# Attention and a gelu layer on one core: the first layer's matmuls of batches 1 to 6 in quarters of the array

## The chip, the cores and the metric

The kernel runs on one core of one Trainium2 chip. A core has a matrix engine, TensorE (PE in the profile, with PEld for its weight loads), and four others: VectorE (DVE), ScalarE (ACT), GpSimd (POOL) and SyncE (SP), which here issues most of the DMAs. Each engine works through its own queue of instructions in order; they wait for one another by semaphores. The metric is the time of one execution on the device, in microseconds.

## What is computed

```python
def _attn_ref(q, k, v, g_q, g_k):            # q, k, v: (8, 12, 448, 64)
    q_n, k_n = (rmsnorm(q, g_q), rmsnorm(k, g_k))
    scores = scale * np.matmul(q_n, k_n.transpose(0, 1, 3, 2))
    attn = np.exp(scores - max) ; attn = attn / sum
    return np.matmul(attn, v)

def _moe_ref(x, w_in, w_out):                # x: (3584, 768), w_in: (768, 2048), w_out: (2048, 768)
    h = x @ w_in
    g = 0.5 * h * (1.0 + np.tanh(c * (h + 0.044715 * h * h * h)))
    return g @ w_out
```

Eight batches of twelve heads go through attention, with q and k normalised; the 8 x 448 rows that come out, of 12 x 64 = 768 features, go through two dense layers with a gelu between them. The matmuls take bf16.

## The kernel before

The batches follow one another. For each there are three kinds of work on TensorE:

- **Attention.** A unit (`unit`, L334) makes the scores of one chunk of four heads and one tile of 64 keys, in four 64x64 quarters of the array, and ScalarE takes their exponential (L338). `products` (L383) makes, also in quarters, the sums of the exponentials and their product with v. VectorE divides (`turned`, `recips`, `quad_x`, L392 to L409) and leaves `xT[b]`, 128 rows by 6 chunks by 448 columns.
- **First layer.** `mm1_pair` (L500) multiplies `w_in` with `xT[b]`. The 2048 features are 16 tiles of 128, taken in 8 pairs; for each tile 6 matmuls with the whole 128x128 array and 448 columns run, one for each chunk `c`. A pair has its own two banks of PSUM. When both of its tiles are done, ScalarE takes the gelu (L513) into `g`. The last pair is done tile by tile, with a gelu for each, of 448 columns.
- **Second layer.** `mm2_quarters` (L443) multiplies `g` with `w_out`, in quarters of the array with 384 columns, for two half tiles of output at once. It runs over the upper and the lower 64 rows in two passes: in the first pass (p = 0) the one output takes rows 0 to 63 and the other 64 to 127, in the second pass (p = 1) the other way round. Between the passes stands a no-operation on SyncE (L452) that waits for the last matmul of the first pass; the first matmul of the second pass waits for it. For the last batch `mm2_last` (L474) uses the whole array.

The order is written by hand. `attention` (L540) runs a list of steps: U is a unit, d and a are one step of the second layer of the batch before (its result copied out by VectorE or ScalarE), A a sum of exponentials, s, t, r, x and q the steps to `xT`, E the gelu's table, m0 and m1 the first two pairs of the first layer, but only their first four chunks (`early`), as `xT` of the last two comes from q2. `first_two` does the same for the first two batches, from a longer list. Behind the steps the loop at L875 does the rest of the first layer: the last two chunks (`late`) of the first two pairs, then the six other pairs. At each tile number f functions of `plan` (L595) are called, which put other work into the engines' queues: POOL's normalisation of the next batch's q and k (`normed`), its transposes by DMA on SP (`dma_trans`, L315), loads (L126), squares of the batch after that on ScalarE (L170) and their sums on VectorE (L177).

PSUM is used as four pairs of banks (s0, s1, t0, t1), handed out in turn by `pair` and put back by `give`; whoever takes a pair waits until its last reader is done.

Of the kernel before, what the change touches and what calls it, by code (L numbers as in the profile page):

```python
# [11 lines left out]
AF = mybir.ActivationFunctionType  # L12
# [5 lines left out]
def kernel(  # L18
# [52 lines left out]
    def pair(name):  # L71
        t = idle_pairs.pop(0)
        if not whole:
            idle_pairs.append(t)
        return t
# [441 lines left out]
            give(h)  # L517

    early, late = range(HP - 2), range(HP - 2, HP)

    def m2_parts(b):
        tiles = range(3) if b % 2 == 0 else range(3, 7)
# [17 lines left out]
    def attention(b, m2, side, ends):  # L540


        units = [(c, t) for c in range(NCH) for t in range(NT)]
        firsts = (0, 3, 6, 9, 11, 13, 16, 18, 21)
        if b % 2 == 0:
            steps = (
# [4 lines left out]
            )  # L551
        else:
            steps = (
# [4 lines left out]
            )  # L558
        u, added_to, early_pairs = 0, 0, 0

        for step in steps.split():
            kind, n = step.rstrip("0123456789"), int(step.strip("UAsxtrqmEad") or 1)
            if kind == "U":
                if u in firsts:
                    for fn in side.get(firsts.index(u), ()):
                        fn()
                unit(b, *units[u])
                u += 1
            elif kind in ("a", "d"):
                for _ in range(n):  # L570
                    m2.pop(0)(nc.scalar.copy if kind == "a" else nc.vector.tensor_copy)
            elif kind == "A":
                for _ in range(n):
                    key_sums(b, *units[added_to])
                    added_to += 1
            elif kind == "s":
                products(b, n, 0)
            elif kind == "t":
                turned()
            elif kind == "r":  # L580
                recips()
            elif kind == "x":
                products(b, n, 1)
            elif kind == "q":
                quad_x(b, n)
            elif kind == "m":
                mm1_pair(n, early, b)
                early_pairs += 1
            elif kind == "E":
                for fn in ends:  # L590
                    fn()
                nc.scalar.preload_act_table_set(GELU_SET)
        return early_pairs
# [130 lines left out]
    def first_two(steps, m2):  # L724
# [3 lines left out]
        for step in steps.split():  # L728
# [27 lines left out]
            elif kind == "U":  # L756
                for _ in range(many):
                    unit(b, *units[u])
                    u += 1
            elif kind in ("a", "d"):  # L760
                for _ in range(many):
                    m2.pop(0)(nc.scalar.copy if kind == "a" else nc.vector.tensor_copy)
            elif kind == "A":
                for _ in range(many):
                    key_sums(b, *units[added_to])
                    added_to += 1
            elif kind in ("s", "x"):
                lo, hi = map(int, rest[1]) if rest[1:] else (0, NT)
                products(b, int(rest[0]), int(kind == "x"), lo, hi)
            elif kind == "q":  # L770
                quad_x(b, int(rest[0]))
            elif kind == "m":
                cs = {"e": early, "l": late}[rest[1]] if rest[1:] else range(HP)
                mm1_pair(int(rest[0]), cs, b)
            elif kind == "h":
                mm1_pair(int(rest[0]), range(HP), b, range(int(rest[1]), int(rest[1]) + 1))
            elif kind == "y":
                idle(many, warm()[:, :168])
            elif kind == "z":
                idle(many, warm())  # L780
            elif kind == "w":
                idle(many, ps_m.tile([128, 512], F32, tag="mm", name="w")[:, :S])
            elif kind == "V":
                load_v(int(rest[0]), 2 * int(rest[1]), 2)
            elif kind == "VV":
                load_v(int(rest[0]), 0, HP)
            elif kind == "VR":
                load_v(int(rest[0]), 2, 4)
            elif kind == "WF":
                w_in_part(0, int(rest[0]), 1)  # L790
            elif kind == "OO":
                w_out_part(int(rest[0]))
            elif kind == "W":
                w_in_part(*map(int, rest[0]))
            elif kind == "Y":
                w_in_rows(*map(int, rest[0]))
            elif kind == "O":
                w_out_part(*map(int, rest[0]), 2)
            elif kind == "gn":
                gain(*map(int, rest[0]))  # L800
            elif kind == "PS":
                b, u = 1, 0
                m2 += m2_parts(0)
                whole.append(True)
            elif kind == "PT":
                whole_psum()
            else:
                {"t": turned, "r": recips, "gp": gain_products, "gc": gains, "gm": bound, "sh": shifted,
                 "rel": released,
                 "rA": lambda: rsqrt(0, 0, q_only, (0,), slice(0, NT), twice=True),  # L810
                 "rB": lambda: rsqrt(0, 0, k_only, (1,), t_first),
                 "rC": lambda: rsqrt(0, 0, k_only, (1,), t_rest),
                 "r1": lambda: rsqrt(0, 1, near=(0, 1), also=(1,)),
                 "r2": lambda: rsqrt(0, 2, near=(1,)),
                 "N1": lambda: rsqrt_newton(1),
                 "rE": lambda: rsqrt(2, slice(0, NCH - 1)),
                 "eG": lambda: nc.scalar.preload_act_table_set(GELU_SET),
                 "eE": lambda: nc.scalar.preload_act_table_set(EXP_SET)}[kind]()
# [27 lines left out]
            )    , m2)  # L846
    begun = 2
    for b in range(1, B):
# [23 lines left out]
        if b + 1 < B:  # L872
            side.append((0, lambda: gain(b + 1, 2)))
        m1 = plan(*m1)
        for f in range(nf):  # L875
            if f + 1 == nf:
                for j in range(2):
                    mm1_pair(f // 2, range(HP), b, range(j, j + 1))
# [46 lines left out]
```

## Time and profile before

| what | us |
|---|---|
| median of three runs | 397.67 |
| their lowest and highest | 396.62, 398.26 |
| the profiled execution | 396.55 |
| its span, from the first to the last instruction | 394.4 |

The lines of the profile have the engine, the line of the kernel (L500), the operation, the tiles that it writes and reads, the part of the array (128*128 or 64*64), the shape and the count. A timeline starts each line with the start in us from the span's beginning and the length of the merged instructions; in square brackets stands the idle time of the engine before them and what ended it. A chain's lines are start, length, engine, tile, line and count. A window's line has the stretch and its length, the busy time and count of PE, PEld, DVE, ACT and POOL, the granted clock, the DMA share and GB/s. A matmul's record lasts longer than the distance to the next one's start, so the pace is read from starts.

### The profile page before, as it was taken

Reading aid. Unit: us, or ns where it says so; the run is one execution under the profiler, and the core shown is the slowest. Engines: PE = TensorE matmul, PEld = TensorE weight load, DVE = VectorE, ACT = ScalarE, POOL = GpSimd, SP = SyncE. Lnnn points to the kernel's source line nnn. Section 1 sums busy time; section 2 is a strip of 40 time slices with the busy share of each in tenths; the row PEclk is TensorE's granted clock in tenths of the full one; section 3 lists DMA queues with packets and bytes.
Section 4 is the critical chain, followed back from the end, with each engine's and each line's share of the span. In section 5 each row is a group of like instructions: output and inputs, shape, how many; then the busy total and the mean of one; then the engine's idle time right before and its main releaser. Section 6 shows DMA issues by size and latency. Waiting matters only on the chain.

```text
span 394.4 us, 12746 instructions
## 1 busy us (share of the span) xinstructions
PE 386.4 (98%) x5679; PEld 247.4 (63%) x5679; DVE 250.0 (63%) x384; ACT 276.4 (70%) x347; POOL 127.7 (32%) x107
## 2 busy tenths in 40 slices
PE   7989999999999999999999999999999999999996
PEld 6455567845666558855666557865666557865564
DVE  5999548896698267954599367963599505980010
ACT  6995389466995689847996579857898259854300
POOL 5995501874305440092203640073301800000000
PEclk9999999999999999999999999999999999999999
DMA  8999994989833947169731959249622611220033
GB/s 282 258 226 218 205 182 118 322 167 272 193 94 70 265 70 211 44 139 230 165 82 42 199 133 216 69 91 249 101 67 59 118 24 42 62 65 0 0 82 80
DMA packets 65594, 54.36 MB, mean 138 GB/s; under 512 B 37380, under 2 KB 60548, under 8 KB 65540
## 3 DMA queue, kind: packets, MB, share of 16 engines
q1 hardware_dynamic: 53184, 41.48, 41.5%
q0 software_dynamic: 12128, 11.80, 19.0%
q8 instruction: 44, 0.72, 0.8%
q10 hardware_dynamic: 228, 0.28, 0.3%
q14 instruction: 10, 0.08, 0.1%
HBM read 45.61 MB, written 11.01 MB: 144 GB/s over the span
## 4 chain that ended last, share of the span: by engine, by line
PE 93%; ACT 3%; DVE 1%; DMA 1%; issue 0%; DVEq 0%; SPq 0%
PE s L443 21%; PE s L500 19%; PE t L500 17%; PE t L443 11%; PE t L383 6%; PE t L334 4%; PE s L334 4%; PE t L474 3%; PE s L383 3%; ACT ex L338 3%; PE s L474 2%; PE tp L297 1%; PE o L383 1%; DMA rawq<-in_q_dram 1%; PE hh L500 1%; DVE nrmq L279 0%
## 5 line engine op out<-in xcount | busy, mean ns | idle before, releaser
L500 PEld LDWEIGHTS <-win 128*128 128x128 bf16 x768 | 74.3, 98 | 70.9 <-issue 3.0
L443 PEld LDWEIGHTS <-g 64*64 64x64 bf16 x3072 | 97.6, 107 | 32.8 <-SPq L452 2.9
L443 PE MATMUL s<-wout,g 64*64 64x384 bf16 x2048 | 102.7, 323 | 0.1
L338 ACT ACTIVATE ex<-t,shift 128x896 bf16<-128x896 f32 x86 | 84.2, 1013 | 3.7 <-PE t L334 2.0
L338 ACT ACTIVATE ex<-s,shift 128x896 bf16<-128x896 f32 x82 | 80.5, 1014 | 6.2 <-PE s L334 3.4
L500 PE MATMUL s<-xT,win 128*128 128x448 bf16 x402 | 81.5, 353 | 0.0
L177 DVE TENSOR_REDUCE ss<-sq 128x14 f32<-128x896 f32 (+3 forms) x45 | 44.4, 997 | 49.2 <-ACT sq L170 43.4
L500 PE MATMUL t<-xT,win 128*128 128x448 bf16 x354 | 71.6, 353 | 0.0
L513 ACT ACTIVATE g<-s 128x896 bf16<-128x896 f32 (+1 forms) x38 | 31.3, 828 | 37.5 <-PE s L500 37.5
L513 ACT ACTIVATE g<-t 128x896 bf16<-128x896 f32 (+1 forms) x33 | 27.5, 837 | 36.0 <-PE t L500 35.9
L443 PE MATMUL t<-wout,g 64*64 64x384 bf16 x1024 | 52.7, 323 | 0.0
L665 POOL COPY mark<-es 1x1 bf16<-1x1 bf16 x5 | 0.9, 178 | 115.4 <-DVE es L357 115.4
L279 POOL TENSOR_TENSOR nrmk<-rawk,rinv 128x896 bf16<-128x896 f32 (+1 forms) x21 | 34.6, 1648 | 5.9 <-DVE o L246 5.9
L279 POOL TENSOR_TENSOR nrmq<-rawq,rinv 128x896 bf16<-128x896 f32 (+1 forms) x21 | 34.5, 1645 | 3.3 <-ACT rinv L209 1.8
L334 PEld LDWEIGHTS <-kT 64*64 64x64 bf16 x672 | 23.4, 106 | 14.4 <-issue 5.4
L172 POOL TENSOR_TENSOR sq<-rawq 128x896 f32<-128x896 f32 (+1 forms) x10 | 15.3, 1534 | 52.9 <-DVE ss L177 26.8
L334 PE MATMUL s<-qT,kT 64*64 64x448 bf16 x328 | 29.8, 355 | 1.9 <-ACT ex L338 1.5
L334 PE MATMUL t<-qT,kT 64*64 64x448 bf16 x344 | 31.5, 350 | 0.0
L383 PEld LDWEIGHTS <-vb 64*64 64x64 bf16 x672 | 22.9, 107 | 8.0 <-issue 0.2
L401 DVE STREAM_TRANSPOSE rb<-rc 128x896 f32<-128x896 f32 x24 | 26.7, 1112 | 0.8
L360 DVE TENSOR_TENSOR e<-ex 128x896 bf16<-128x896 bf16 x32 | 19.4, 605 | 5.7 <-ACT ex L338 5.7
L383 PE MATMUL t<-ex,vb 64*64 64x448 bf16 x420 | 22.7, 349 | 0.0
(109 smaller groups left out, 386.0 us busy)
## 6 DMA issues: line engine op xcount, KB each, us to landing
out_dram<-osb SPq DMA_DIRECT2D x54, 192.0 KB, 2.8
rawq<-in_q_dram SPq DMA_DIRECT2D x23, 448.0 KB, 4.3
rawk<-in_k_dram SPq DMA_DIRECT2D x23, 448.0 KB, 5.5
vb<-in_v_dram POOLq DMA_DIRECT2D x8, 672.0 KB, 7.1
wout<-in_moe_w_out_dram POOLq DMA_DIRECT2D x2, 1536.0 KB, 22.9
win<-in_moe_w_in_dram POOLq DMA_DIRECT2D x6, 256.0 KB, 10.3
win<-in_moe_w_in_dram POOLq DMA_DIRECT2D x4, 384.0 KB, 13.0
kT<-nrmk SPq DMA_TRANSPOSE x19, 4.6
```

The lines of the kernel that those rows point to most:

```text
L172: eng.tensor_mul(sq, raw, raw)
L177: nc.vector.reduce_sum(sss[b][:, c, "qk".index(n), hs, ts], squares(b, c, n, hs, ts), axis=AX.X)
L279: eng.tensor_mul(nrms[n, b, c][:, ts].rearrange("p t a d -> p a t d"), raws[n, b, c][:, :, ts], root[:, :, ts].to_broadcast([P, 2, m, D]),)
L334: nc.tensor.matmul(sc[r * R:(r + 1) * R, a, :S], kT[rs, c, t, r], qT[b][rs, c, :, r], start=True, stop=True,)
L338: nc.scalar.activation(ex[:, t], sc[:, :, :S], AF.Exp, scale=scale, bias=shift)
L360: nc.vector.tensor_add(e2, ex[:, t - 1], ex[:, t])
L383: nc.tensor.matmul(o[r][a * D:(a + 1) * D], vb[b % 2][rs, 2 * c + a, i] if what else ones[rs], es[i][rs, a], start=(i == 0), stop=(i == n ...
L401: nc.vector.transpose(rb.rearrange("p r s -> p (r s)"), rc.to_broadcast([128, 2 * S // 32, 32]))
L443: done = nc.tensor.matmul(o[c * R:(c + 1) * R, n, :HD], g[rs, f, i * 128 + c * R:i * 128 + (c + 1) * R], wout[rs, f, half * HD:(half + 1) ...
L474: nc.tensor.matmul(o, g[:, f, i * 128:(i + 1) * 128], wout[:, f, lo:hi], start=(f == 0), stop=(f == nf - 1),)
L500: nc.tensor.matmul(h[j][:, :S] if type(h) is list else h[:, j, :S], win[:, c, f * 128:(f + 1) * 128], xT[b][:, c], start=(c == 0), stop=(c ...
L513: nc.scalar.activation(g[:, 2 * i + lo:2 * i + js[-1] + 1, (b % 2) * S:(b % 2 + 1) * S], h[:, lo:js[-1] + 1, :S], AF.Gelu_apprx_tanh)
```

## The change

For batches 1 to 6 the first layer is done by `mm1_quarters` in place of `mm1_pair`: four 64x64 quarters at once, two for each of the pair's two tiles of features. In the first pass tile 2i uses the lower rows of each chunk and tile 2i + 1 the upper; in the second pass (p = 1) they swap. Between the passes stands a no-operation on ScalarE (on GpSimd for the early and late chunks of batch 1) that waits for the last matmul of the first pass; the first matmul of the second pass waits for it. `mm1_begin` does the early chunks of the first two pairs: pass 0 of pair 0, pass 0 of pair 1, then pass 1 of each. `mm1_rest` does the late chunks the other way round, and for the six other pairs sets the first pass of a pair ahead of the second pass of the pair before it. The last pair is cut by columns, two halves of 224, each with a pair of banks and a gelu of its own. The functions of the plan keep their numbers, but are called at other places among the matmuls. In the list for batch 1, the square of k and the load of v for batch 2 move ahead of the first pairs. Batches 0 and 7 stay as they were.

```diff
+    def mm1_quarters(b, i, p, cs, begins=False, swaps=False, ends=False, cols=slice(0, S)):
+        key = (i, cols.start)
+        if begins:
+            hs1[key] = pair("hh")
+        h, turn = hs1[key], turns.pop(key, None)
+        for c in cs:
+            for n in range(2):
+                rs, f = slice((n ^ p) * R, (n ^ p) * R + R), 2 * i + n
+                for m in range(2):
+                    done = nc.tensor.matmul(
+                        h[m * R:(m + 1) * R, n, cols],
+                        win[rs, c, f * 128 + m * R:f * 128 + (m + 1) * R],
+                        xT[b][rs, c, cols],
+                        start=(begins and c == cs[0]), stop=(ends and c == cs[-1]),
+                    )
+                    if turn:
+                        tc.add_manual_dep(done.ins, turn.ins.name, SYNC)
+                        turn = None
+        if swaps:
+            eng = nc.gpsimd if b == 1 and len(cs) < HP else nc.scalar
+            turn = eng.nop(nofuse=True)
+            tc.add_manual_dep(turn.ins, done.ins.name, SYNC)
+            turns[key] = turn
+        if ends:
...
+            nc.scalar.activation(g[...], h[:, :, cols], AF.Gelu_apprx_tanh)
+            give(h)
+
+    def mm1_begin(b, n):
+        if n == 0:
+            mm1_quarters(b, 0, 0, early, begins=True, swaps=True)
+            mm1_quarters(b, 1, 0, early, begins=True, swaps=True)
+        else:
+            mm1_quarters(b, 0, 1, early)
+            mm1_quarters(b, 1, 1, early)
+
+    def mm1_rest(b, after):
+        every, last, done = range(HP), nf // 2 - 1, []
+
+        def through(i, p, cs, **at):
+            for fn in after.get(2 * len(done), ()):
+                fn()
+            mm1_quarters(b, i, p, cs, ends=True, **at)
+            for fn in after.get(2 * len(done) + 1, ()):
+                fn()
+            done.append(i)
+
+        mm1_quarters(b, 0, 1, late, swaps=True)
+        mm1_quarters(b, 1, 1, late, swaps=True)
+        through(0, 0, late)
+        through(1, 0, late)
+        mm1_quarters(b, 2, 0, every, begins=True, swaps=True)
+        for i in range(3, last):
+            mm1_quarters(b, i, 0, every, begins=True, swaps=True)
+            through(i - 1, 1, every)
+        sides = [slice(0, S // 2), slice(S // 2, S)]
+        mm1_quarters(b, last, 0, every, begins=True, swaps=True, cols=sides[0])
+        through(last - 1, 1, every)
+        mm1_quarters(b, last, 0, every, begins=True, swaps=True, cols=sides[1])
...
+        for cols in sides:
+            mm1_quarters(b, last, 1, every, ends=True, cols=cols)
...
-                "q.2 d a2 eG m.0.e a2 m.1.e sq.k22.P VV.2"
+                "q.2 d a2 eG sq.k22.P VV.2 m.0.e a2 m.1.e"
...
+        if b + 1 < B:
+            mm1_rest(b, m1)
```

More of the change, by code (lines that the diff above doesn't have):

```diff
@@ new lines, in mm1_begin @@
+    def mm1_begin(b, n):
[26 more added lines that the diff above has]
+        mm1_quarters(b, last, 0, every, begins=True, swaps=True, cols=sides[1])
+        for fn in after.get(2 * last, ()):
+            fn()
+        for cols in sides:
+            mm1_quarters(b, last, 1, every, ends=True, cols=cols)
+        for fn in after.get(2 * last + 1, ()):
+            fn()
@@ L585, in attention @@
                 quad_x(b, n)
+            elif kind == "m" and b + 1 < B:
+                mm1_begin(b, n)
             elif kind == "m":
@@ L773, in first_two @@
                 cs = {"e": early, "l": late}[rest[1]] if rest[1:] else range(HP)
-                mm1_pair(int(rest[0]), cs, b)
+                if b == 1:
+                    mm1_begin(b, int(rest[0]))
+                else:
+                    mm1_pair(int(rest[0]), cs, b)
             elif kind == "h":
@@ L874 @@
         m1 = plan(*m1)
-        for f in range(nf):
+        if b + 1 < B:
+            mm1_rest(b, m1)
+        for f in range(nf if b + 1 == B else 0):
             if f + 1 == nf:
```

6 lines of the change are left out of this document (added).

## The prediction

> **What bounds the kernel.** I read the page's busy shares and its chain first.
>
> ```profile
> span 394.4 us, 12746 instructions
> PE 386.4 (98%) x5679; PEld 247.4 (63%) x5679; DVE 250.0 (63%) x384; ACT 276.4 (70%) x347; POOL 127.7 (32%) x107
> ...
> PE 93%; ACT 3%; DVE 1%; DMA 1%; issue 0%; DVEq 0%; SPq 0%
> ```
>
> PE is busy for 98% of the span and is 93% of the chain, so a change counts by what it does to the spacing of PE's starts. "Busy" itself hides gaps, because a matmul's record runs on past the start of the next. Then the chain in order of time (start, length, engine, line, count), whose lengths are start to start:
>
> ```profile
> 123.56 1.32 PE s L383 x28
> ...
> 166.29 2.60 PE s L443 x64
> ...
> 175.06 4.54 PE t L500 x24
> ...
> 369.73 2.60 PE t L474 x16
> ```
>
> This is the first thing that matters. L474 is the whole array and L443 the quarters, both with 384 columns: 16 whole matmuls take 2.60 us, and 64 quarter matmuls, which is 16 groups of four, also take 2.60 us: 0.1625 us each way. With 448 columns a whole matmul takes 4.54 / 24 = 0.1892 us, and a group of quarters (L383) 1.32 / 7 = 0.1886 us. So quarters stream no faster than the whole array; what the change can win lies only at the edges. The timeline of PE shows them, for batches 1, 2 and 3:
>
> ```profile
> 78.24 1.08 PE L443 MATMUL s<-wout,g 64*64 64x384 bf16 x20
> 79.26 1.69 PE L500 MATMUL t<-xT,win 128*128 128x448 bf16 x8
> 80.87 0.52 PE L443 MATMUL s<-wout,g 64*64 64x384 bf16 x8
> ...
> 98.29 1.14 PE L443 MATMUL s<-wout,g 64*64 64x384 bf16 x24
> ...
> 124.72 0.49 PE L443 MATMUL t<-wout,g 64*64 64x384 bf16 x8
> 125.14 1.69 PE L500 MATMUL t<-xT,win 128*128 128x448 bf16 x8
> ...
> 143.41 0.68 PE L443 MATMUL t<-wout,g 64*64 64x384 bf16 x12
> 143.92 0.36 PE L334 MATMUL t<-qT,kT 64*64 64x448 bf16 x4
> ...
> 149.77 0.36 PE L334 MATMUL s<-qT,kT 64*64 64x448 bf16 x4
> 150.03 0.38 PE L334 MATMUL t<-qT,kT 64*64 64x448 bf16 x4
> ...
> 168.89 1.52 PE L383 MATMUL t<-ex,vb 64*64 64x448 bf16 x28
> 170.34 1.50 PE L500 MATMUL s<-xT,win 128*128 128x448 bf16 x7
> ...
> 188.60 0.38 PE L334 MATMUL s<-qT,kT 64*64 64x448 bf16 x4
> 188.82 0.49 PE L443 MATMUL t<-wout,g 64*64 64x384 bf16 x8
> ```
>
> **What goes: the changes of array shape.** Batch 2: two groups from 124.72 end at 124.72 + 2 x 0.1625 = 125.05. From there to 143.92 are 18.87 us for 96 whole matmuls (18.16) and three groups (0.49), 18.65 us of work. The difference, 0.22 us, is the price of one change to the whole array and one back, near 0.11 each. Batch 3: from 168.89 + 7 x 0.189 = 170.21 to 188.82 are 18.61 us for 18.16 + 0.19; the difference is 0.26. Batch 6 looks like batch 2:
>
> ```profile
> 306.20:324.47 18.27, 18.27 (x101) 9.31 (x97) 5.19 (x7) 6.86 (x8) 8.06 (x5) 1.00 0.40 77
> ```
>
> (The window from the first whole matmul to the first quarter behind them, 18.27 us for 18.16 of stream, as 125.14 to 143.41 is in batch 2.) I take batch 4 for like 2 and batch 5 for like 3. Batch 1 has four changes, because two groups of the second layer stand between its first two pairs: 78.24 + 5 x 0.1625 = 79.05 to 98.29 is 19.24 us for 18.16 + 0.33 + 0.19 = 18.68, so 0.56 at most; I take 4 x 0.11 = 0.44, as in the others. Sum 0.44 + 5 x 0.22 = 1.54 us, at most 0.56 + 3 x 0.22 + 2 x 0.26 = 1.74.
>
> **What of it does not come through.** Behind batches 2, 4 and 6 PE already waits: the unit at 150.03 starts 0.26 after the one at 149.77 instead of 0.19. ScalarE sets that.
>
> ```profile
> 129.14 0.92 ACT L513 ACTIVATE g<-t 128x896 bf16<-128x896 f32 x1 [5.13 <-PE t L500]
> ...
> 139.79 1.03 ACT L170 ACTIVATE sq<-rawk 128x448 f32<-128x448 f32 x2
> ...
> 143.52 0.55 ACT L513 ACTIVATE g<-s 128x448 bf16<-128x448 f32 x1 [0.59 <-PE s L500]
> 144.08 1.28 ACT L888 ACT_TABLE_LOAD   x1
> 145.37 1.01 ACT L338 ACTIVATE ex<-t,shift 128x896 bf16<-128x896 f32 x1
> ...
> 148.95 1.03 ACT L338 ACTIVATE ex<-t,shift 128x896 bf16<-128x896 f32 x1
> ```
>
> The last gelu, the table load and the exponentials run without a break from 143.52 on and hang on the end of the first layer, which ends with as large a gelu as before (448 columns). PE leaves that layer 0.11 to 0.12 earlier against this chain and waits as much longer: 3 x 0.12 = 0.36 us is lost. Behind the odd batches no such gap stands in the timeline (188.60 to 188.82 is the change of shape alone); there I charge nothing, at worst another 0.36.
>
> **What is added: half-width groups.** The last pair of tiles is done in two halves of 224 columns, 24 groups in place of 12 of 448.
>
> ```profile
> 387.77 1.48 PE L474 MATMUL s<-wout,g 128*128 128x192 bf16 x16
> 389.09 1.48 PE L474 MATMUL t<-wout,g 128*128 128x192 bf16 x16
> ```
>
> 16 matmuls of 192 columns start in 1.32 us, 0.0825 each; with 0.1625 at 384 that is 2.5 ns and 0.4167 ns a column, so 0.0958 at 224. 24 x 0.0958 - 12 x 0.1892 = +0.03 us a batch, +0.18 in all. That is for the whole array, one weight load per start; quarters need four loads in 0.096 us. The nearest quarter row is 0.1625 for 384 columns, and its stream alone explains that, so it bounds from above only: 6 x 24 x (0.1625 - 0.0958) = +9.6 us. I take the stream, because nothing in the rows of 384 and 448 columns shows a quarter group slower than its stream. [...]
>
> **What is added: the swaps.** Each pair of tiles now does one half of its rows, then waits until a no-operation has seen the last matmul, then does the other. The second layer already does this with SyncE:
>
> ```profile
> 107.28 0.49 PE L443 MATMUL t<-wout,g 64*64 64x384 bf16 x8
> 107.60 0.36 PE L334 MATMUL t<-qT,kT 64*64 64x448 bf16 x4
> 107.88 0.52 PE L443 MATMUL t<-wout,g 64*64 64x384 bf16 x8
> ...
> 107.88 0.31 PEld L443 LDWEIGHTS <-g 64*64 64x64 bf16 x12 [0.32 <-SPq L452]
> ```
>
> The last group before that swap starts at 107.28 + 0.16 = 107.44, the first behind it at 107.88: 0.44 us round, 0.47 with 448 columns. The shortest cover in the new order is at the late chunks, two groups on each side: 0.19 of its own + 2 x 0.19 = 0.57. So 0.10 to spare, price 0; without cover a swap would cost 0.47 - 0.19 = 0.28, and with four short ones a batch 24 x 0.28 = 6.7 us bounds this from above. At the early chunks four groups (0.76) cover it, later six (1.13). ScalarE is free there (5.13 us idle before the gelu of 129.14). Its queue behind a swap (gelus, squares) is held up to the end of a first half: the squares come some six groups, 1.1 us, later, with them VectorE's sums of squares and gains. VectorE sat idle for 1.31 us in that place before its next copy:
>
> ```profile
> 126.90 1.09 DVE L409 TENSOR_TENSOR xT<-s,rb 128x896 bf16<-128x896 f32 x1
> ...
> 146.63 0.96 DVE L457 COPY osb<-t 128x768 f32<-128x768 f32 x1 [1.31 <-PE t L443]
> ```
>
> So price 0, with 0.2 left; if that cover goes, a later copy holds a pair of banks, at most 0.2 us for two batches. The late chunks need xT, done at 126.90 + 1.09 = 127.99; PE is there at 125.05 + 16 x 0.189 = 128.08, where it was at 128.18: price 0, at most 0.05 a batch.
>
> In batch 1 the four swaps at the early and late chunks stand in POOL's queue, behind a square and the issue of v that were moved ahead of them, and ahead of the normalisation of batch 2:
>
> ```profile
> 78.85 0.88 POOL L148 DMA_DIRECT2D vb<-in_v_dram  x1
> 81.50 1.68 POOL L279 TENSOR_TENSOR nrmq<-rawq,rinv 128x896 bf16<-128x896 f32 x1 [1.76 <-ACT rinv L209]
> ...
> 86.34 1.31 SPq L315 DMA_TRANSPOSE qT<-nrmq  x1
> 87.75 1.26 SPq L315 DMA_TRANSPOSE kT<-nrmk  x1
> ```
>
> POOL is done with the issue at 79.73, before PE's first swap near 80.1. The normalisation starts when the second late half is done, 79.05 + 20 x 0.189 + 0.33 and some 0.4 for the last matmul to end, near 83.6, 2.1 us later; q is ready at 85.3 and k at 87.0, still before SP comes to their transposes (86.34, 87.75). SP's and POOL's orders are otherwise the same. Price 0; at worst the 2.1 us reach batch 2, whose first unit is 10 us away.
>
> **Sum.** -1.54 + 0.36 + 0.18 = -1.00 us. The profiled execution took 396.55 us, so 395.55; it was 1.12 below the median of the runs, 397.67, so against that 396.7.
>
> **Rivals.**
>
> *Half-width groups fed too slowly (ends slower).* Place: the 24 groups of 224 columns of each batch. Four loads and four matmuls must be issued in 0.096 us, where no row has more than eight in 0.1625. Against it: nothing holds the rows of 384 columns above their stream; for it: nothing shows denser ones. The gain is gone at 0.0958 + 1.00 / 144 = 0.103 us a group, and it is 0.5% slower than before (2 us) from 0.117. Halfway between the bounds, 0.129, it costs 4.8 us: 396.7 + 4.8 = 401.5. [...]
>
> *ScalarE carries out the no-operation only when its running work is done.* Then the swap of the second half-width waits for the gelu of tile pair 6. Pair 5 ends its second half 18 groups' worth, 3.4 us, before the layer's end; 0.2 later its gelu runs (0.92), then two squares (1.03), then pair 6's gelu (0.92), over 0.3 us before the end; the swap is needed three groups, 0.57, plus a hand-over before it: 0.35 late in the five batches with squares, +1.7 us: 398.4. [...]
>
> *All of it is lost.* ScalarE or VectorE bind behind every batch: -1.54 + 0.72 + 0.18 + 0.5 for the small covers = -0.1: 397.5.
>
> *All of it comes through.* No wait grows, and the larger edges hold: -1.74 + 0.18 = -1.6: 396.1.
>
> **Chances.** Forecast 0.50 (its own range 396.2 to 397.3), slow halves 0.20, late no-operation 0.12, all lost 0.08, all through 0.10. 0.5% is 2.0 us, about what a measurement of this kernel tells from no change (its three runs spread over 1.64). No term reaches 2.0 downward, so faster needs several to be larger than read: 0.12, out of the last case and the spread. Slower is the upper part of the slow halves and some of the uncovered swaps: 0.23. The rest, 0.65, is the same. The range goes from 395.0 (all through, less 1.1 of spread) to 400.5 (halves at 0.122), which leaves out under 2 in 10.
>
> **What would show it.** Groups of 448 columns at 0.189; no step of 0.1 where PE enters or leaves the first layer; half-width groups at 0.096; no wait of PE for ACT's or POOL's sequencer; the gap near 150 grown from 0.07 to 0.19. I am wrong if half-width groups stand above 0.103, if waits for the sequencers sum to more than 0.5 us, or if quarters stream unlike 0.189.

## The result, and the profile after

The changed kernel is slower by a little: 399.35 us median of 22 runs (396.79 to 401.80) against 397.45 (396.26 to 399.51) for the kernel before, a ratio of 1.0046 with a 95% interval from 1.0027 to 1.0065. The forecast was 396.7. The time lies in the range, on the other side of the kernel before. The profiled execution took 399.25 us.

The page of the changed kernel (its span, the busy shares, the queue that brings PE's instructions, the chain by engine):

```profile
span 397.2 us, 16850 instructions
...
PE 388.5 (98%) x7695; PEld 287.6 (72%) x7695; DVE 248.5 (63%) x384; ACT 276.6 (70%) x347; POOL 127.5 (32%) x107
...
q8 instruction: 60, 0.98, 1.0%
...
PE 87%; ACT 3%; DMA 3%; POOL 3%; DVE 1%; SPq 1%; issue 1%; POOLq 0%; DVEq 0%
```

and the same queue on the page of the kernel before:

```profile
q8 instruction: 44, 0.72, 0.8%
```

PE fell from 93% of the chain to 87%; DMA rose from 1% to 3%, "issue" from 0% to 1%, SP's queue from 0% to 1%, and POOL is new on it with 3%. PE's instructions, matmuls and weight loads, went from 2 x 5679 to 2 x 7695, and their packets, 16 KB each, from 44 to 60: one packet for some 256 instructions (2 x 7695 / 60 = 256.5).

Where PE has no long wait, what was forecast came out. A line of the chain in batch 2, then the timelines of PE and ACT at the end of batch 4's first layer:

```profile
131.75 3.40 PE s L532 x72
```

```profile
235.45 0.75 PE L532 MATMUL s<-xT,win 64*64 64x224 bf16 x24
236.02 0.75 PE L532 MATMUL t<-xT,win 64*64 64x224 bf16 x24
236.60 0.66 PE L443 MATMUL t<-wout,g 64*64 64x384 bf16 x12
...
242.94 0.37 PE L334 MATMUL s<-qT,kT 64*64 64x448 bf16 x4
243.33 0.38 PE L334 MATMUL t<-qT,kT 64*64 64x448 bf16 x4
```

```profile
235.13 0.91 ACT L548 ACTIVATE g<-s 128x896 bf16<-128x896 f32 x1
236.24 0.55 ACT L548 ACTIVATE g<-s 128x448 bf16<-128x448 f32 x1 [0.20 <-PE s L532]
236.82 0.55 ACT L548 ACTIVATE g<-t 128x448 bf16<-128x448 f32 x1
237.38 1.28 ACT L968 ACT_TABLE_LOAD   x1
```

A group of 448 columns takes 3.40 / 18 = 0.189 us, one of 224 columns (236.60 - 236.02) / 6 = 0.097. Both steps of shape are gone: the groups ahead of the layer and behind it follow at their pace (in batch 4 two groups of 384 columns start at 218.08 and the layer at 218.41, the last six of 224 at 236.02 and the second layer at 236.60). The gap near the seventh unit is 0.39 - 0.19 = 0.20 us where 0.07 stood. Behind batch 3 the kernel before had a gap too, 0.28 - 0.19 = 0.09 us:

```profile
198.13 0.36 PE L334 MATMUL t<-qT,kT 64*64 64x448 bf16 x4
198.41 1.17 PE L443 MATMUL s<-wout,g 64*64 64x384 bf16 x24
```

The loss stands elsewhere. PE from the end of batch 1's first layer on:

```profile
96.18 0.89 PE L532 MATMUL t<-xT,win 64*64 64x224 bf16 x24
97.34 0.77 PE L532 MATMUL s<-xT,win 64*64 64x224 bf16 x24 [0.27 <-ACTq L543]
...
98.52 0.36 PE L334 MATMUL t<-qT,kT 64*64 64x448 bf16 x4
99.15 1.17 PE L443 MATMUL s<-wout,g 64*64 64x384 bf16 x24 [0.27 <-ACT g L548]
...
102.53 1.01 PE L443 MATMUL s<-wout,g 64*64 64x384 bf16 x20
103.74 0.68 PE L443 MATMUL s<-wout,g 64*64 64x384 bf16 x12 [0.21 <-issue]
```

Six groups of 224 columns from 96.18 should end at 96.76, but the next group starts at 97.34, released by the no-operation in ACT's queue (L543); the unit from 98.52 should be followed at 98.71, but the next matmul starts at 99.15. Then there is a pause of another kind: before 103.74 PE waits for "issue", which no semaphore ended (0.40 us more than the pace). One of 0.62 us, of the same kind, stands at 158.9:

```profile
158.89 0.38 PE L334 MATMUL s<-qT,kT 64*64 64x448 bf16 x2
159.69 0.38 PE L334 MATMUL s<-qT,kT 64*64 64x448 bf16 x2 [0.42 <-issue]
```

It falls between the four matmuls of one group, the first two of which had already started.

From the first matmul of batch 1's first layer to the end the kernel before took 315.16 us and the changed one 317.81. Of these 2.65 us, PE's starts (pace of the group taken off) give 0.97 to the two waits for ACT, 1.22 to four pauses without a semaphore, and 0.37 to one at 107.4, where a copy by VectorE stands behind the sum of a square whose load came late. The 0.09 left over is the balance of small waits of 0.1 to 0.2 and of what the steps of shape saved. (The stretch ahead of batch 1's first layer does much the same work in all versions but took from 79.0 to 81.2 us in the profiled executions, so these are compared from that layer on.)

### The profile page after: what moved, and what is told of

Its sections match the earlier page's. It is cut to its first block, busy times and chain, and to the rows that moved or that the text cites. A ratio compares the mean times of both kernels' runs of the same rounds, so it can differ in the third digit from the quotient of the medians.

```text
span 397.2 us, 16850 instructions
## 1 busy us (share of the span) xinstructions
PE 388.5 (98%) x7695; PEld 287.6 (72%) x7695; DVE 248.5 (63%) x384; ACT 276.6 (70%) x347; POOL 127.5 (32%) x107
## 4 chain that ended last, share of the span: by engine, by line
PE 87%; ACT 3%; DMA 3%; POOL 3%; DVE 1%; SPq 1%; issue 1%; POOLq 0%; DVEq 0%
PE t L443 19%; PE s L532 13%; PE t L532 11%; PE s L443 11%; PE s L500 6%; PE s L383 6%; PE s L334 5%; PE t L334 3%; PE t L383 3%; PE t L474 3%; PE s L474 3%; PE t L500 3%; ACT ex L338 3%; DMA rawk<-in_k_dram 2%; DMA rawq<-in_q_dram 1%; POOL nrmq L279 1%
## 5 line engine op out<-in xcount | busy, mean ns | idle before, releaser
L338 ACT ACTIVATE ex<-s,shift 128x896 bf16<-128x896 f32 x104 | 100.9, 1013 | 6.1 <-PE s L334 3.6
L532 PEld LDWEIGHTS <-win 64*64 64x64 bf16 x2592 | 86.1, 107 | 24.7 <-ACTq L543 2.2
L443 PE MATMUL t<-wout,g 64*64 64x384 bf16 x1920 | 98.3, 323 | 0.0
L532 PE MATMUL s<-xT,win 64*64 64x448 bf16 (+1 forms) x1344 | 67.3, 329 | 0.3 <-ACTq L543 0.3
L338 ACT ACTIVATE ex<-t,shift 128x896 bf16<-128x896 f32 x64 | 63.9, 1014 | 5.1 <-issue 2.8
L532 PE MATMUL t<-xT,win 64*64 64x448 bf16 (+1 forms) x1248 | 62.7, 328 | 0.0
L443 PE MATMUL s<-wout,g 64*64 64x384 bf16 x1152 | 58.9, 323 | 0.6 <-ACT g L548 0.3
L500 PEld LDWEIGHTS <-win 128*128 128x128 bf16 x192 | 18.5, 98 | 17.3 <-issue 0.7
L500 PE MATMUL s<-xT,win 128*128 128x448 bf16 x126 | 25.0, 352 | 0.0
L383 PE MATMUL s<-ex,vb 64*64 64x448 bf16 x448 | 24.5, 349 | 0.0
```

What stands on the lines that cost most here:

```text
L338: nc.scalar.activation(ex[:, t], sc[:, :, :S], AF.Exp, scale=scale, bias=shift)
L383: nc.tensor.matmul(o[r][a * D:(a + 1) * D], vb[b % 2][rs, 2 * c + a, i] if what else ones[rs], es[i][rs, a], start=(i == 0), stop=(i == n ...
L443: done = nc.tensor.matmul(o[c * R:(c + 1) * R, n, :HD], g[rs, f, i * 128 + c * R:i * 128 + (c + 1) * R], wout[rs, f, half * HD:(half + 1) ...
L500: nc.tensor.matmul(h[j][:, :S] if type(h) is list else h[:, j, :S], win[:, c, f * 128:(f + 1) * 128], xT[b][:, c], start=(c == 0), stop=(c ...
L532: done = nc.tensor.matmul(h[m * R:(m + 1) * R, n, cols], win[rs, c, f * 128 + m * R:f * 128 + (m + 1) * R], xT[b][rs, c, cols], start=(beg ...
```

## The experiments

Four theories stood at the start. A: GpSimd, held by the swaps in batch 1, normalises batch 2 later, and with it come SP's transposes and loads. B: the quarters cost something in every batch. C: the stalls without a semaphore are PE waiting for instructions. D: ScalarE's chain behind the first layer swallows the gain.

**e1: batch 1 whole again.**

```diff
-                if b == 1:
-                    mm1_begin(b, int(rest[0]))
-                else:
-                    mm1_pair(int(rest[0]), cs, b)
+                mm1_pair(int(rest[0]), cs, b)
...
-        if b + 1 < B:
+        if 1 < b < B - 1:
             mm1_rest(b, m1)
-        for f in range(nf if b + 1 == B else 0):
+        for f in range(nf if b in (1, B - 1) else 0):
```

> Batch 1 does its first layer with the whole array again, in the list order of before; batches 2 to 6 stay in quarters. Theory A (the loss is in batch 1: GpSimd's normalisation of batch 2 is held by the swaps, and its transposes and the loads behind it come late): from the end of batch 1's first layer to the start of batch 2's 27.0 us, as before, in place of 28.5; batch 1's first-layer stage 18.8 in place of 19.2; the normalisation of q starts at 81.5. In time some 1.7 us less than the changed kernel's, 397.4 to 397.7, the same as before. Theory B (the loss lies with the quarters in every batch, ScalarE and the swaps): the time keeps at least 5/6 of the loss, 398.9 or more. Theory C (stalls of PE without a semaphore, where its instruction stream comes late): those stalls move, as batch 1 has 312 matmuls fewer, but stay, and 0.5 to 1.1 us of the loss with them.

398.42 us, 1.0023 [0.9999, 1.0048]. The waits for ACT are gone, and batch 1's layer takes 18.82 us as before. Two pauses without a semaphore stand in the trace, at 112.8 and 249.9, together 1.31 us. From batch 1's first layer on it took 316.20 us; without the two pauses that is 314.89, a little below the kernel before. By the medians about half of the loss belongs to batch 1, but the interval reaches from none of the loss to all of it. In this execution the rest is what theory C says, and a cost of theory B's kind isn't there.

**e2 and e3: the hold on GpSimd, taken away and put alone.**

```diff
-            eng = nc.gpsimd if b == 1 and len(cs) < HP else nc.scalar
+            eng = nc.gpsimd if b == 1 and cs is early else nc.scalar
```

> In batch 1 the swaps at the late chunks go to ScalarE; those at the early chunks stay on GpSimd. All batches in quarters. Theory A: the normalisation of q starts near 81.5 in place of 83.9, SP's loads (3,1) and (3,2) are issued as before (89.1, 93.7 us), and PE's stalls at 96.7, 98.5 and 107.4 (together some 1.4 us) go; from batch 1 to batch 2 27.0 to 27.3 us in place of 28.5; time 397.9 to 398.3. If the late loads come from the transposes of SP and not from the hold on GpSimd, the stalls stay and the time is the changed kernel's, 399.3. Theory C: the stall of 0.5 us at 103.2 stays, as no matmul is added or taken away; theory A says nothing of it.

The kernel before, with the hold alone:

```diff
...
+        if b == 1:
+            mm1_pair(0, late, b)
+            hold = nc.gpsimd.nop(nofuse=True)
+            tc.add_manual_dep(hold.ins, held_by["mm"].ins.name, SYNC)
...
```

> The kernel before, whole array throughout, with one no-operation on GpSimd in batch 1 ahead of the normalisation of batch 2, which waits for the last late matmul of the first pair of tiles (it ends near 82.9; so the normalisation starts 1.2 to 2 us later than at 81.5). Theory A: the same lateness alone, without quarters, costs 0.7 to 1.7 us: loads later than 93.7, stalls of PE between 96 and 108, the gap from batch 1 to batch 2 28 or more in place of 26.9; time 398.2 to 399.2. Rival: the hold is harmless by itself (the transposes had 1 us and more to spare) and it is the swaps on ScalarE's queue or the moved square and load of v that cost: time as before, 397.5, gap 26.9.

e2: 399.71 us, 1.0047 [1.0026, 1.0069], as the changed kernel. e3: 397.57 us, 0.9991 [0.9972, 1.0010], as the kernel before. The hold is really there in e3; the timelines of POOL in e3 and in e2:

```profile
84.97 1.68 POOL L279 TENSOR_TENSOR nrmq<-rawq,rinv 128x896 bf16<-128x896 f32 x1 [4.76 <-PE t L500]
```

```profile
82.72 1.68 POOL L279 TENSOR_TENSOR nrmq<-rawq,rinv 128x896 bf16<-128x896 f32 x1 [2.30 <-ACT rinv L209]
```

Counted from batch 1's first layer (80.24 and 80.55) that is 4.73 and 2.17 us; it was 2.24 in the kernel before and 4.58 in the changed one. The same lateness alone costs nothing, and without it nothing is won: theory A falls. In e2's execution the waits for ACT were absent, and 2.08 us of pauses without a semaphore had come, in four places (103.3, 143.7, 159.0, 192.3).

**e4: the last pair in one piece.**

```diff
-        sides = [slice(0, S // 2), slice(S // 2, S)]
+        sides = [slice(0, S)]
```

> As the changed kernel, but the last pair of tiles is done in one piece of 448 columns, with one gelu of 896 at the end in place of two of 448. Theory D (ScalarE's chain of last gelu, table load and exponentials sets the start of the next batch's stretch, and swallows what the first layer gains): the chain starts on the same end and has a gelu longer by some 0.37 us, so PE waits that much more behind each of the batches 2 to 6: the two gaps near 150 us and at 198 grow by 0.3 to 0.4 each, 1.5 to 1.9 us in all; time 400.8 to 401.2. If the chain has slack, the half-width groups are saved (0.03 us a batch) and nothing else moves: 399.2.

399.25 us, 1.0046 [1.0029, 1.0063]. The timelines of ACT and PE behind batch 4:

```profile
235.56 0.92 ACT L548 ACTIVATE g<-t 128x896 bf16<-128x896 f32 x1 [0.22 <-PE t L532]
236.50 1.28 ACT L967 ACT_TABLE_LOAD   x1
```

```profile
235.34 0.66 PE L443 MATMUL s<-wout,g 64*64 64x384 bf16 x12
...
238.85 0.38 PE L334 MATMUL s<-qT,kT 64*64 64x448 bf16 x4 [0.20 <-ACT ex L338]
```

The table load starts 236.50 - 235.34 = 1.16 us behind the layer, in the changed kernel 237.38 - 236.60 = 0.78, and PE now waits for an exponential. From batch to batch the gaps between the first layers are 27.44 and 27.29 us where the changed kernel has 27.10 and 27.03: theory D holds, by 0.26 to 0.34 a batch. The time did not follow. In the profiled execution no pause without a semaphore stood behind 80 us, so there two effects of opposite sign cancel; that they do so in the median too is likely but not shown.

**e5 and e6: without most of the loads** (those of v stay).

```diff
     def load(b, c, n, parts=1, engs=(nc.sync,)):
+        if b > 2:
+            raws[n, b, c] = raws[n, 2, c]
+            return []
```

> The changed kernel without the loads of q and k for batches 3 to 7 (left out: those batches use q and k of batch 2; every other operation is there). Theory C, as the four runs so far bear it out (PE stalls without a semaphore, always at instruction 193 of a block of 256; the 16 KB packet with the next block begins 3 us and more after the block boundary when some 900 KB of loads move in these 3 us, and within 0.4 us of it when none move): from batch 2 on no packet begins more than 2 us late and no such stall stands behind 100 us; the spread of the times shrinks. Against the same cut of the kernel before (next run) the changed one is then 0 to 1 us slower, what is left being waits with a semaphore. Rival (the stalls come from the denser instructions alone, not from the loads): the stalls stay at 1 to 2.5 us a run and the difference to the cut kernel before stays near 1.9 us.

> The kernel before with the same loads left out (batches 3 to 7 use q and k of batch 2). Every theory: 396.5 to 397.5, hardly faster than the kernel before, as its first layer takes 15 to 20 us for a block of 256 instructions and shows no such stall behind 76 us.

396.81 us for the changed kernel without these loads, 396.48 for the one before: 0.33 apart in place of 1.90. Each median is known to about 0.2%, and four of e5's twelve executions still took 398.1 to 399.7 us, against one of e6's with 398.2; so the medians point the way that theory C says without settling it, and the spread shrank less than expected. The windows from batch 1's first layer to the end, of e5 and then of e6:

```profile
79.64:394.14 314.50, 310.77 (x6615) 233.15 (x6604) 188.46 (x278) 219.50 (x273) 82.00 (x57) 1.00 0.43 76
```

```profile
79.02:394.06 315.04, 311.32 (x4596) 197.81 (x4592) 191.60 (x279) 219.72 (x273) 82.39 (x57) 1.00 0.38 75
```

In this stretch e5, the quarters, is 0.54 us shorter. Neither trace has a pause without a semaphore there, nor a wait for ACT at the end of batch 1. The instructions of e5 are as dense as in the changed kernel, so density alone is not the cause: it takes the loads too. One point of the expectation missed: a packet began 3.4 us behind its boundary at 238 us, beside a load of v, though no pause followed.

**e7: k's loads set apart from q's** (with e2's edit).

```diff
-            m1 += [(4, lambda: loads(b + 2, 1)), (8, lambda: loads(b + 2, 2))]
+            m1 += [
+                (at, lambda c=c, n=n: [go() for go in load(b + 2, c, n)])
+                for at, c, n in ((4, 1, "q"), (6, 1, "k"), (8, 2, "q"), (10, 2, "k"))
+            ]
...
-                side.append((1 if b % 2 else 2, lambda: loads(b + 3, 0)))
+                side += [
+                    ((1 if b % 2 else 2) + i, lambda n=n: [go() for go in load(b + 3, 0, n)])
+                    for i, n in enumerate("qk")
+                ]
```

> As the run with all late swaps of batch 1 on ScalarE, and the loads of q and k for a third of a batch, which are issued back to back, are set apart: k's two tile numbers behind q's in the first layer, and one call later in the attention. Theory C: no more than some 460 KB stand ahead of a packet of instructions, which then begins at most 2 us behind the block boundary, in place of 3 to 4; stalls at instruction 193 of a block go in batches 2 to 7 (one near 75 us, whose loads are not moved, may stay); with theory A's stalls gone too, 397.3 to 398.2, 1.2 to 2.4 us below the 399.7 of that run. If the loads do not set it, or if a late load makes a new wait, 399.7 or more.

398.85 us, 1.0031 [1.0009, 1.0054]: between the two ranges expected. The edit did only half of what it says. SP's queue in e7:

```profile
130.22 0.58 SPq L126 DMA_DIRECT2D rawq<-in_q_dram  x1
130.85 0.48 SPq L126 DMA_DIRECT2D rawk<-in_k_dram  x1
...
152.19 0.38 SPq L126 DMA_DIRECT2D rawq<-in_q_dram  x1
157.65 0.59 SPq L126 DMA_DIRECT2D rawk<-in_k_dram  x1
```

In the first layer SP works off a backlog of transposes, and the loads leave back to back wherever they stand in the order; only in the attention (152.19 and 157.65) did they come apart. There the pause near 159, 0.62 us in the changed kernel and 0.52 in e2, is gone. Two of 0.25 and 0.11 stay beside loads that still run in pairs. The waits for ACT in batch 1, 1.09 us, stand here although GpSimd isn't held:

```profile
98.12 0.77 PE L532 MATMUL s<-xT,win 64*64 64x224 bf16 x24 [0.45 <-ACTq L543]
```

**e8: a shorter last gelu** (with e2's edit).

```diff
-        sides = [slice(0, S // 2), slice(S // 2, S)]
+        sides = [slice(0, 320), slice(320, S)]
```

> As the run with all late swaps of batch 1 on ScalarE, with the last pair cut into 320 and 128 columns in place of 224 and 224. Theory D (ScalarE's chain behind the first layer swallows the gain): the last gelu is shorter by about 0.1 us, and the stalls near 151.8, 242.9 and 333.5 (0.20 to 0.21) and 288.4 (0.10) shrink by about 0.1 each; 0.3 to 0.6 us less in the trace. Without it nothing moves. In time 399.2 to 399.6 with it, 399.7 without, since the stalls without a semaphore stay.

399.97 us, 1.0060 [1.0039, 1.0081]. A miss. PE and ACT behind batch 4:

```profile
235.93 0.51 PE L532 MATMUL t<-xT,win 64*64 64x128 bf16 x24
236.26 0.66 PE L443 MATMUL t<-wout,g 64*64 64x384 bf16 x12
```

```profile
236.15 0.70 ACT L548 ACTIVATE g<-s 128x640 bf16<-128x640 f32 x1 [0.23 <-PE s L532]
236.75 0.38 ACT L548 ACTIVATE g<-t 128x256 bf16<-128x256 f32 x1
237.15 1.28 ACT L968 ACT_TABLE_LOAD   x1
```

The load of the table starts 0.89 us behind the layer, later than the 0.78 of the even cut: the gelu of the first part can now start only 0.11 us before the layer's end, and the second waits for it. The two last gelus run one after the other, so their sum counts, not the last one.

**What holds the swap in batch 1.** With theory A gone, the cause of the waits for ACT is in ACT's own queue. ACT in the changed kernel, and in the kernel before:

```profile
94.26 1.04 ACT L170 ACTIVATE sq<-rawq 128x448 f32<-128x448 f32 x2 [0.78 <-DMA rawq<-in_q_dram]
95.21 0.90 ACT L548 ACTIVATE g<-t 128x896 bf16<-128x896 f32 x1
97.25 1.04 ACT L170 ACTIVATE sq<-rawk 128x448 f32<-128x448 f32 x2 [1.14 <-DMA rawk<-in_k_dram]
98.20 1.33 ACT L548 ACTIVATE g<-s 128x896 bf16<-128x896 f32 x2
```

```profile
95.21 1.03 ACT L170 ACTIVATE sq<-rawk 128x448 f32<-128x448 f32 x2
```

The square waits until 97.25 for the load of k, and behind it in the queue stand the no-operation for the last pair, which PE then gets at 97.34, and the last gelus. In the kernel before (the last line) the load was there in time, so the square did not wait, and no such no-operation stood behind it. Call that A'.

**e9 to e11: A' and the loads, singly and together.**

```diff
+            if b == 1:
+                for n in "qk":
+                    m1.append((13, lambda n=n: square(b + 2, 1, n, nc.gpsimd)))
+                    side.append((0, lambda n=n: total(b + 2, 1, n)))
-            for c, at in ((0, 4), (1, 9)):
+            for c, at in ((0, 4), (1, 9))[:1 if b == 1 else 2]:
```

That is e10; e11 adds e7's loads to it, e9 adds them to e1.

> As the changed kernel, but in batch 1 the squares of the second third of batch 3 go from ScalarE to GpSimd, ahead of those of the last third, and their sums behind the first layer. Theory A' (in batch 1 the swap of the last pair waits in ScalarE's queue behind a square that waits for rawk): PE's stalls at 96.7 (0.53) and 98.5 (0.44) go and ScalarE's wait for rawk with them; about 1 us less, 398.3 to 398.7. Rival (the last gelus come late for another reason, or the hold on GpSimd is the cause after all): the stalls stay, 399.4. The packets of instructions begin late as before.

> Both remedies with all batches in quarters: squares of batch 1 on GpSimd, loads of k set apart. Theories A' and C together: 397.3 to 398.0, the same as before, with no PE stall over 0.3 us behind 85 us but what GpSimd's longer queue may bring; at most 0.5 us less than that, since ScalarE's chain behind the first layer (last gelus end 0.84 us behind the layer in place of 0.67) gives back what the shape changes saved. If quarters had a cost of their own, 398.4 or more.

> Batch 1 with the whole array and the loads of k set apart from those of q. Theory C+A' (two causes make the loss: instruction packets that begin late behind the loads, and, in batch 1 alone, ScalarE's swap of the last pair queued behind a square that waits for a load): both are gone, no PE stall over 0.3 us behind 85 us, 397.3 to 397.9 us, the same as before within 0.1%, and some 0.6 to 1 us below the 398.4 of batch 1 whole alone. If there is a third cause in batches 2 to 6, 398.4 or more.

e10: 399.06 us, 1.0032 [1.0009, 1.0056]. PE at the end of batch 1, and at the next boundary of a block:

```profile
96.79 0.80 PE L532 MATMUL t<-xT,win 64*64 64x224 bf16 x24
97.37 0.80 PE L532 MATMUL s<-xT,win 64*64 64x224 bf16 x24
...
98.52 0.41 PE L334 MATMUL t<-qT,kT 64*64 64x448 bf16 x4
98.71 1.04 PE L443 MATMUL s<-wout,g 64*64 64x384 bf16 x20
...
103.85 0.65 PE L443 MATMUL s<-wout,g 64*64 64x384 bf16 x9 [0.93 <-issue]
```

The groups follow at 0.097 without a break and the unit of 98.52 is followed at 98.71: with the squares out of ACT's queue the waits are gone, as A' says. That is not luck with the load, which came as late as in the changed kernel, as POOL shows:

```profile
97.53 1.68 POOL L172 TENSOR_TENSOR sq<-rawk 128x896 f32<-128x896 f32 x1 [1.20 <-DMA rawk<-in_k_dram]
```

Now it is GpSimd that waits for it, and nothing that PE needs soon stands behind. A pause of 1.13 us for instructions took back what that brought in this execution. From batch 1 on 315.82 us, without the pause 314.69. The median misses the range expected, 398.3 to 398.7.

e11: 398.70 us, 1.0032 [1.0011, 1.0054]; no wait for ACT, and two pauses for instructions, 0.61 and 0.89 us, beside loads that did not come apart. e9: 398.41 us, 1.0015 [0.9997, 1.0034]; the profiled execution has neither of the two and takes 315.01 us from batch 1 on, 0.15 below the kernel before. Of the changed versions with all loads it is the only one with neither, and this execution shows no third cause. But both medians miss the range expected of them and lie where the expectations put a third cause or a cost of the quarters themselves, at 398.4 or more. The profiled executions of e9 to e12 are 0.8 to 1.5 us faster than the medians of their kernels; what the other executions lost was not traced, so a third cause is not excluded.

**e12: the blocks shifted.**

```diff
+            elif kind == "Y48":
+                idle(112, warm()[:, :72])
...
-                "y48 sq.q00.A.h0 to.q00.h0 sq.q00.A.h1 z3 to.q00.h1 sq.k00.A.t0 "
+                "Y48 sq.q00.A.h0 to.q00.h0 sq.q00.A.h1 z3 to.q00.h1 sq.k00.A.t0 "
```

> As the changed kernel, with 64 idle matmuls more in the warm-up (112 of 72 columns for 48 of 168), so that every later block of 256 instructions of PE ends 128 instructions earlier in the work. Theory C: the stalls without a semaphore stay at instruction 193 of a block; in the work they leave the places where they stood (103.2 and 158.9 us, counted from batch 1's first layer) by some 3 us, and may be fewer or more, as other boundaries now fall into the loads; time 398 to 401. If the stalls belong to the work (a bank, a tile, a late operand that the trace does not show), they stay at the same matmuls.

399.14 us, 1.0031 [1.0013, 1.0049]. PE's longest pause in this execution:

```profile
109.99 0.82 PE L443 MATMUL t<-wout,g 64*64 64x384 bf16 x16
112.10 0.68 PE L443 MATMUL t<-wout,g 64*64 64x384 bf16 x12 [1.29 <-issue]
```

It is PE's instruction 3777; 3777 = 14 x 256 + 193. The places of 103.2 and 158.9 run through. The pauses follow the count of instructions, not the work. The time is within the range expected.

**The packets.** Taken together, the traces of the ten changed versions with all loads tell theory C's mechanism. PE's pauses of this kind stand at instruction 193 of a block of 256 (3265, 5057, 5825 in the changed kernel; 3009 and 9409 in e1; 3265, 5825, 7361 in e2), and end 1.2 to 1.7 us after a 16 KB packet of the instruction queue has landed, which itself takes some 0.9 us. (The one at 3009 in e1 the profile puts down to an exponential; it too ends 1.4 us behind its packet.) Where under 100 KB of data move in the 3 us behind a boundary, the packet begins 0.28 us behind it on average (125 boundaries between 60 and 345 us); with 100 to 400 KB 0.51 (185), with 400 to 700 KB 1.63 (91), with more 2.39 (107). The latest began 4.7 us behind its boundary; it is the one ahead of e12's pause. The DMA view of the changed kernel shows one that begins late: between the boundary at 97.76 us and 101.2 only the loads and transposes of q and k move, all in queue q1, then the packet comes.

```profile
DMA packets 1230, 1.09 MB, mean 319 GB/s; under 512 B 718, under 2 KB 1230, under 8 KB 1230
...
q1 hardware_dynamic: 1230, 1.09, 129.3%
```

```profile
q1 hardware_dynamic: 110, 0.03, 158.7%
q8 instruction: 1, 0.02, 5.7%
```

(The second window is 101.2 to 102.2.) PE ran dry before 103.74. In quarters a block of the first layer lasts 6.0 us, 4.0 to 4.5 with the half-width groups at its end; with the whole array it lasted 15 to 20 us. A block of attention lasts 5.4 to 5.5 us, in the kernel before as in the changed one. A packet that begins 3.3 us late or more, with 2.3 us until its instructions run, just fills a block of 5.4 to 6.0 us and left a pause, from 0.03 us up, in 16 of 23 cases. A longer block takes it unseen: in the kernel before one began 3.2 us late at 74.7 us, in a block of 8.9 us that reaches into the first layer, and PE did not pause.

That does not make the denser first layer the cause of every pause. The blocks ahead of some pauses hold first layer (all of it ahead of the 0.14 us at 143.8, most of it ahead of e11's 0.89). But those ahead of the 0.62 us at 158.9, of e1's two, of e8's 0.82 and of e12's 1.46 hold none of it, only attention and the second layer's steps between, the same matmuls in both kernels. In the kernel before, packets behind 78 us began up to 3.0 us late and no pause followed; in e3, the whole array too, two began 3.8 and 3.4 us late, and PE paused 0.35 us at 75.2 and 0.16 at 111.9, both at instruction 193. How late a packet is depends on where its boundary falls in the loads, and every instruction added shifts the boundaries. No run shifts the count in the kernel before, as e12 does in the changed one. So how much of these pauses is the price of more instructions, and how much the place where the boundaries happened to fall, is not shown.

## Why the prediction came out wrong

Two steps failed: the price 0 for the swaps, in batch 1, and a sum without a term for bringing the instructions. What ScalarE gives back was too small besides. Term by term:

- **The pace** (groups of 448 columns at 0.189, of 224 at 0.0958): right, 0.189 and 0.097. The rival of slow half-width groups, with a chance of 0.20, falls. Denser starts keep the pace as well: e8's groups of 128 columns take (236.26 - 235.93) / 6 = 0.055 us for four matmuls.
- **The changes of shape, -1.54**: gone, as said. In e5 and e6, batch 1's layer is 18.52 us against 18.82 and the others 18.19 against 18.26. Counted from its first matmul on, the layer holds three of batch 1's four steps and one of the others' two, each sum less the 0.03 for the halves: 0.30 and 0.08 were forecast for that part.
- **What ScalarE gives back, +0.36**: too small. The gap behind even batches grew as forecast (0.07 to 0.20), but the odd ones give back as much: behind batch 3 the changed kernel has waits of 0.10 and 0.11 us at 197.8 and 200.9, where the kernel before had only one, 0.09, at 198.1, behind the last line that the prediction read (188.82). From batch 3 to batch 5 the changed kernel takes 90.54 us, the kernel before 90.53. The prediction's "at worst another 0.36" was near the true case. Its reason, that the chain hangs on "as large a gelu as before", left out that two gelus of this size now come together. With both terms, -0.54 was left in e5 and e6 of the -1.00 forecast: right in kind, off by half.
- **Price 0 for the swaps: the first step that failed.** It asked what stands behind a no-operation in ScalarE's queue and not what stands ahead of it. In batch 1 a square ahead of it waits for a load: 0.97 us in the profiled execution, 1.09 and 1.14 in e7 and e8, nothing in e2 and e12, where the load came in time, nor in e10, where it came late and the square was out of the way. In batches 2 to 6 of the changed kernel no wait for ScalarE's queue stands, so there the price was right.
- **Price 0 for GpSimd's hold in batch 1**: right; e3 has it alone and takes as long as before.
- **The no-operation waits for running work** (rival, 0.12): falls. In the ACT rows of batch 4 a gelu runs from 235.13 to 236.04 while the swap of the last half must be seen; PE goes on at 236.02, 0.02 us before that gelu ends, without a break.
- **The term that was not there: instructions, the second step that failed.** The sum counted what each instruction takes on PE and not that 4032 more must be brought, in 16 more packets, which begin late beside the loads (2.39 us behind their boundary on average where over 700 KB move, 0.28 where under 100 KB do). The pauses are 1.22 us in the profiled execution and 0 to 2.08 in those of the other versions. The runs also differ more, 5.0 us from lowest to highest against 3.25 before. That late packets make these pauses is shown; how much of them would be there without the added instructions is not, as said above.

With both kinds of waits taken off, e1, e2, e5, e7 and e9 to e12 need 314.5 to 315.0 us from batch 1 on, and the kernel before 315.16; e8 needs 315.4 and the changed kernel 315.6, where smaller waits follow those in batch 1. The gain is there in these executions, a few tenths at most, and is paid several times over.

Open is how the 1.9 us of the medians divide. e1 and e9 leave 1.0 and 0.8 of it, but the intervals reach about 0.2% to each side, and the pauses differ from execution to execution of the same program. Why a packet waits behind loads (one engine, one ring, or the memory) no trace shows; that the loads of q and k make it late, the counts above and e5 show. Not explained either is why the load of k that the square in batch 1 needs took 4.8 to 5.3 us from its issue to its last semaphore in some executions (the kernel before, e1, e2, e3, e9, e11, e12) and 6.2 to 6.7 in others (the changed kernel, e4, e7, e8, e10); it came late in the second group alone.

## What to carry to other kernels

Count instructions as a resource: here the same work in four times as many instructions shortened the time that one block of 256 lasts in the first layer to 6.0 us, where it was 15 to 20, and moved all later block boundaries, and where over 700 KB moved behind a boundary the next packet began 2.39 us late on average; look for pauses of PE that no semaphore ended, at a fixed place in every 256 (here instruction 193). When a wait is put into an engine's queue, look ahead of it as well as behind it: here a square that waited 1.14 us for the load of k held the no-operation and the gelus that followed. And where the profiled executions of one kernel carry different pauses, take the pauses off one by one before comparing: e4 and the changed kernel have the same median, and their profiled executions lose the time in different places.

## What the runs showed of the hardware beside that

In e8 groups of four quarter matmuls of 128 columns follow at 0.055 us, which is what the prediction's 2.5 ns and 0.4167 ns a column give for one matmul: starts of single quarters are some 14 ns apart on average. A packet was late beside another load too: in e5, without most of those of q and k, one still began 3.4 us behind its boundary at 238 us, while 0.53 MB of a load of v moved that GpSimd had issued at 235.37.
